# Empty half-steps before the turnings of gated values, later transpositions for block 0, and parts beside a unit's first product with V

## The chip, the cores and the metric

The kernel runs on one core of a Trainium2 chip. The metric is the device time of one execution in microseconds, as a median of runs. Below, PE is the matrix engine, PEld its weight loads, DVE the vector engine, ACT the scalar engine, POOL the general engine, and SP the engine that issues the DMAs.

## The reference

One layer: an adaptive layer norm, attention with 32 query heads and one shared key and value head of 16 columns, and a gated feed-forward. S is 2048, D is 512, F is 1792, all in float32.

```python
mod = (silu(c) @ w_mod)               # six rows of 512: sa, ca, ga, sb, cb, gb
h = layernorm(x) * (1 + ca) + sa
q, k, v = h @ wq, h @ wk, h @ wv      # 32 heads of 16; one k, one v of 16
p = softmax(q @ k.T / 4)              # per head, 2048 x 2048
x = x + ga * ((p @ v) @ wo)
h = layernorm(x) * (1 + cb) + sb
x = x + gb * ((sigmoid(h @ w_gate) * (h @ w_up)) @ w_down)
```

## The kernel before

**Units and half-steps.** After a prologue of some 108 us, attention runs in 32 units: 8 blocks of 256 queries times 4 groups of 8 heads. A unit has 16 steps, one for each block of 128 keys, and a step has two half-steps. So the loop has 1024 half-steps. Half-step 12 of unit 5 is written 5.12 below. In each half-step PE makes, in the order `ORDER`, two score tiles for the row maxima (`a0`, `a1`, tile `sa`), two transposed score tiles (`s0`, `s1`, tile `st`), and the product of an older block's exponentials with V (`c`, tile `craw`), which runs `LAG` = 2 steps behind. DVE reduces both `sa` tiles to maxima (`mx`), and ACT takes the exponential of both `st` tiles (`P`). The maxima run 84 products ahead of the scores, so the last 42 half-steps have none. `sa` has three buffers and `st` has two. Every matmul of the loop uses a piece of the array of 64 rows by 32 columns, and pieces on both halves of the rows run side by side.

**Parts.** All other matrix work of the layer is cut into parts and put at the end of half-steps: the rest of the queries (`q`), the output projection (`wo`), the gate and up products (`gu`) and the down product (`dn`). A part is one term of a pair of product groups (`Couple`): eight matmuls of 64x32 with 512 columns. A pair of gate and up groups has 24 parts. `places` spreads the parts of a `Couple` over half-steps at a rate, with a weight for each half-step from `weight`. A unit's last product with V stands in half-step 3 of the next unit; ACT then copies `craw` out into `cs`, and the first product of the new unit, in half-step 4, waits for that copy. `weight` gives half-step 3 five parts (`SWAP`) and half-step 4 none, but only for couples at the full rate. Query parts and the parts of block 0 (those marked `slow`) have the same weight everywhere.

**Blocks.** The feed-forward goes by 4 blocks of 512 rows. Block 0 is done in two halves of 256 rows in units 4 to 16, at the lower rate `ERATE`. There the gate and up products come out row-wise (`pgr`). ACT takes the tanh of one part of them, DVE copies the other part, POOL multiplies them into `g`, and a `Turned` piece of four transpositions by PE turns `g` for the down product. Block 0 has 14 of these turnings (stage `gt`). `Transposes` (stage `tr`) turn the normed rows `t` into `h2` before the gate and up products. `pick` takes the next group: a `tr` may start `GAP` steps after the norm was recorded in `marks`, and couples in `spare` fill in where the main list can't go on. When a `Couple` doesn't fit before the end of the loop, it stays over for the tail. The tail follows the last half-step. It does the leftover couples and block 3's feed-forward without attention, with whole-array matmuls (line 185).

**Order on the engines.** PE, DVE, ACT and SP work in the order in which the code is written until the tail. POOL's order is chosen by the scheduler when the kernel is built.

Of the kernel before, what the change touches and what calls it, by code (L numbers as in the profile page):

```python
# [26 lines left out]
NKB = S // P  # L27
# [34 lines left out]

SKIP = 9
GAP = 2
KEPT = 2
RATE = 2.2
QRATE = 1.0
ERATE = 1.65
MOST = 3
SWAP = 5  # L70
WSTEPS = 95
WLAST = 112
WLATE = 2
# [14 lines left out]
def adaln_mqa_glu_kernel(  # L88
# [47 lines left out]
    pinned, first = [True], [True]  # L136
# [50 lines left out]
                self.end(self.bank, False)  # L187

    class Couple:
        slow = False  # L190

        def __init__(self, a, c):
            self.gs, self.stage, self.w, self.n = (a, c), a.stage, a.w, 2 * a.n
# [586 lines left out]
    marks = {}  # L780
# [16 lines left out]
    def ffn_groups(b):  # L797
# [80 lines left out]
        def gu_rows(t, e):  # L878
            at = len(uses) // 2 * (t // 2) + e

            def term(n, rs):
                k, i = divmod(n, 3)
                gw = gws[at]
                h_, w_ = passes(*h2[k], 0, 1)[i]
                return h_[rs, t * P:(t + 1) * P], gw[rs, :, w_:w_ + 3:2, k, :]

            def end(p_, second):
                gs_[t, e] = g_ = t32("g")
                z = p_.rearrange("p (f m n) -> p f m n", f=2, m=2)
                th, u_ = (g_[:, m * QU:(m + 1) * QU].rearrange("p (f n) -> p f n", f=2) for m in range(2))  # L890
                act.activation(th, z[:, :, 0], AF.Tanh, scale=0.5 / (SH * SW))
                dve.tensor_copy(u_, z[:, :, 1])
                pool.tensor_scalar(th, th, 1.0, 1.0, op0=ALU.add, op1=ALU.mult)
                pool.tensor_tensor(th, th, u_, op=ALU.mult)
                marks[b, "g", t // 2, e] = now[0]

            return Group("gu", 12, "pgr", term, end, (lambda: ask(at + GWB)) if t % 2 == 0 else None)

        def turned(u, e):
            pt = bank("pt3")  # L900
            for f in range(2):
                for t in range(2):
                    pe.transpose(pt[:, (2 * f + t) * P:(2 * f + t + 1) * P], gs_[2 * u + t, e][:, f * P:(f + 1) * P], ident)
            h32, hi, lo = t32("h32"), t16("gh"), t16("gl")
            act.activation(h32, pt, AF.Identity)
            pool.tensor_scalar(hi, h32, 1.0, 0.0, op0=ALU.mult, op1=ALU.add)
            pool.tensor_tensor(lo, h32, hi, op=ALU.subtract)
            for f in range(2):
                gT[fs[2 * e + f]] = hi[:, f * QU:(f + 1) * QU], lo[:, f * QU:(f + 1) * QU]
# [30 lines left out]
        def down_group(t, lo, hi):  # L940
            n_ = hi - lo
            t0 = t % 2 if split else t

            def term(n, rs):
                f, i = fs[lo + n // 3], n % 3
                g_, w_ = passes(*gT[f], wdh, wdl)[i]
                return g_[rs, t0 * P:(t0 + 1) * P], w_[rs, f, :]

            def end(p_, second):
                ot = t32("ot")  # L950
                if second:
                    act.activation(ot, p_, AF.Identity)
                    pool.tensor_tensor(ot, ot, mods[5], op=ALU.mult)
                else:
                    dve.tensor_tensor(ot, p_, mods[5], op=ALU.mult)
                if hi < NFC:
                    pool.tensor_tensor(x1[t][0], ot, x1[t][0], op=ALU.add)
                else:
                    pool.tensor_tensor(ot, ot, x1[t][0], op=ALU.add)
                    store = lambda: sp1.dma_start(out[b * QB + t * P:b * QB + (t + 1) * P, :], ot)  # L960
                    if tail:
                        store()
                    else:
                        defer(2 + t % 2, store)

            return Group("dn", 3 * n_, "pd", term, end)
# [3 lines left out]
        if split:  # L970
            halves = []
            for u in range(2):
                gs = [Couple(gu_rows(2 * u, e), gu_rows(2 * u + 1, e)) for e in range(NFC // 2)]
                ts = [Turned(lambda n0, n1, u=u, e=e: turned(u, e), (b, "g", u, e)) for e in range(NFC // 2)]
                seq = [gs[0]]
                for e in range(1, NFC // 2):
                    seq += [gs[e], ts[e - 1]]
                seq += [ts[-1], Couple(down_group(2 * u, 0, NFC), down_group(2 * u + 1, 0, NFC))]
                for z in seq:
                    z.slow = True  # L980
                halves.append([Couple(*wos[2 * u:2 * u + 2]), trs[u], trs[u + 2], *seq])
            return halves
        gs = []
# [67 lines left out]

    def weight(hb, q):
        s, h = divmod(hb, 2)
        t = (s - LAG) % NKB
        if s >= LAG and (t, h) == (0, 0):
            return 0.0
        if (t, h) == (NKB - 1, 1):
            return SWAP / RATE if not q else 1.0  # L1060
        return 1.0 if q else (2 - SWAP / RATE + 2 * (NKB - 1)) / (2 * NKB - 2)

    def places(m, hb, rate, most, skip, part):
        ws = []
        rate, most = rate / part, most / part
        while sum(ws) * rate < m + lead[0] / part - rate / 2 or sum(ws) * most < m:
            ws.append(0.0 if len(ws) < (skip or 0) else weight(hb + len(ws), skip is not None))
        lead[0] += part * (m - rate * sum(ws))
        ends = [round(m * sum(ws[:k + 1]) / sum(ws)) for k in range(len(ws))]
        return [k - z for z, k in zip([0] + ends, ends)]  # L1070
# [3 lines left out]
    def ready(pair, gs, i):  # L1074
        for g in gs:
            g.ready = i * NKB
        return [(pair, g) for g in gs]

    def pick(s):
        if first_rows and s >= (len(units) - NU) * NKB + SKIP:  # L1080
            return first_rows.pop()
        while main and main[0][0] is None:
            n = main.pop(0)[1]
            spare.extend(z[1] for z in main[:n])
            del main[:n]
        if main:
            b, g = main[0]
            if g.stage == "tr":
                ok = (b, g.u) in marks and s >= marks[b, g.u] + GAP
            elif g.stage == "wo":  # L1090
                ok = s >= g.ready + SKIP
            elif g.stage == "gt":
                ok = s >= marks[g.mark] + GAP + 1
            else:
                ok = not spare
            if ok:
                return main.pop(0)[1]
        return spare.pop(0) if spare else None


    def plan(s, hb):
        if run:
            return
        g = pick(s)
        if g is None:
            lead[0] = 0.0
            return
        if g.stage in ("tr", "gt"):
            sizes = [4]
        else:  # L1110
            q = g.stage == "q" and s < FIRST
            light = g.slow
            rate, most = (QRATE, 1) if q else (ERATE, 2) if light else (RATE, MOST)
            sizes = []
            for leg in range(2):
                sizes += places(g.n // 2, hb + len(sizes), rate, most, (3 if leg == 0 else 0) if q else 0 if light else None, g.w)
            if hb + len(sizes) > 2 * len(units) * NKB:
                spare.insert(0, g)
                return
        at = 0  # L1120
        for z in sizes:
            run.append((g, at, at + z))
            at += z
        assert at == g.n, (at, g.n, g.stage)

    def piece(s, h):
        plan(s, 2 * s + h)
        if run:
            g, n0, n1 = run.pop(0)
            if n1 > n0:  # L1130
                g.part(n0, n1)
# [5 lines left out]
    for i, (b, o) in enumerate(units):  # L1137
        if o == 0 and b == NQ - 1:
            ends = ffn_groups(NB - 1)
            first_rows.append(Couple(*ends[0][:2]))  # L1140
# [9 lines left out]
        elif o == 0 and b % 2 == 0 and b > 0:  # L1150
            wos, trs, gs = blocks.pop(b // 2 - 1)
            gs = [Couple(*wos[2:]), trs[1], trs[3], *gs]
            main.extend([*ready(b // 2 - 1, gs[:-KEPT], i), (None, KEPT), *ready(b // 2 - 1, gs[-KEPT:], i)])
        for kb in range(NKB):
            s = i * NKB + kb
# [29 lines left out]
            while wdone < nw:  # L1185
                if wdone < nw - 4 and (wdone + 0.5) * WSTEPS > (s + 1) * (nw - 4):
                    break
# [23 lines left out]
    wos, trs, gs = ends  # L1211
# [44 lines left out]
```

## Time and profile before

| | us |
|---|---|
| median of 3 runs (lowest, highest) | 1713.26 (1713.11, 1713.76) |
| the profiled execution, its own time | 1710.52 |
| the profile's span | 1708.7 |
| PE, DVE, ACT, POOL busy | 1656.0, 1430.7, 1299.5, 605.8 |
| mean granted PE clock | 0.990 |
| copies `cs` that end the units: first and last start | 156.5, 1571.9 |
| row maxima on DVE, 2048 of them | 1287.6 |
| exponentials on ACT, 2048 of them | 1171.4 |

The span leaves out 1.8 us of the profiled execution's own time, and that execution is 2.7 us under the median. A busy PE is not always a PE at its peak: a matmul's record holds its latency (376 ns for the f16 ones) and not only its share of the array, so neighbouring records overlap.

### The profile page before, as it was taken

The page shows a single profiled execution, that of the slowest core. Times are in us where ns is not written, and L with a number is a line of the kernel's source. Part 1 is how long each engine was busy: PE and PEld are TensorE (multiplying, and loading weights), DVE is VectorE, ACT ScalarE, POOL GpSimd, SP SyncE. Part 2 cuts the span into 40 slices and gives each one's busy share as a digit, 9 for nine tenths or more (in the row PEclk, how much of TensorE's full clock was granted, in tenths as well). Part 3 has the DMA queues.
Part 4 walks back from the last instruction along what each step waited for, and adds up shares of the span by engine and source line. Part 5 has one row for each costly group of instructions (what it writes and reads, how often), then busy time and mean ns, then how long its engine had stood idle before and what let it go on. Part 6 is the DMA issues. An engine that isn't in the chain of part 4 may idle for free.

```text
span 1708.7 us, 89331 instructions
## 1 busy us (share of the span) xinstructions
PE 1656.0 (97%) x40446; PEld 1000.3 (59%) x40446; DVE 1430.7 (84%) x2440; ACT 1299.5 (76%) x2361; POOL 605.8 (35%) x808
## 2 busy tenths in 40 slices
PE   6999999999999999999999999999999999999998
PEld 3335555456656656666656666666666676654443
DVE  7799999989999999999999999999999999931411
ACT  5449998878888888888888888888888888885100
POOL 4433556753423022233143322232443232322423
PEclk9989999999999999999999999999999999999999
DMA  7112333422210022210021110111121100111211
GB/s 242 53 61 61 124 116 112 142 71 69 82 52 15 16 77 64 64 27 16 28 73 40 40 37 14 38 39 28 40 77 40 56 24 25 35 54 48 74 49 50
DMA packets 88184, 101.48 MB, mean 59 GB/s; under 512 B 24580, under 2 KB 65532, under 8 KB 87804
## 3 DMA queue, kind: packets, MB, share of 16 engines
q1 hardware_dynamic: 87804, 95.78, 17.6%
q8 instruction: 316, 5.18, 1.3%
q14 instruction: 64, 0.52, 0.1%
HBM read 75.16 MB, written 16.24 MB: 53 GB/s over the span
## 4 chain that ended last, share of the span: by engine, by line
PE 84%; DVE 7%; ACT 3%; POOL 2%; DMA 1%; issue 1%; SPq 1%; POOLq 0%; ACTq 0%; DVEq 0%
PE craw L134 23%; PE sa L134 14%; PE st L134 12%; PE pgu L134 10%; PE pd L134 7%; PE pgr L134 5%; PE pgu L185 4%; DVE mx L134 4%; PE pd L185 3%; PE pq L134 2%; PE po L134 2%; ACT P L134 1%; PE pt L134 1%; SPq L134 1%; DVE h2h L134 1%
## 5 line engine op out<-in xcount | busy, mean ns | idle before, releaser
L134 DVE TENSOR_REDUCE mx<-sa 128x1 f32<-128x512 f32 x2048 | 1287.6, 682 | 85.3 <-PE st L134 43.6
L134 ACT ACTIVATE P<-st 128x512 f32<-128x512 f32 x2048 | 1171.4, 598 | 215.3 <-PE st L134 153.2
L134 PE MATMUL craw<-P,V 64*32 64x512 f32 x8192 | 1098.6, 600 | 1.1 <-ACT cs L134 0.3
L134 PE MATMUL sa<-kp,qp 64*32 64x512 f16 (+1 forms) x7940 | 838.2, 379 | 11.8 <-DVE mx L134 10.9
L134 PE MATMUL st<-qp,kp 64*32 64x512 f16 x8192 | 838.9, 380 | 7.6 <-ACT P L134 6.3
L134 PEld LDWEIGHTS <-kp 64*32 64x32 f16 x8192 | 334.5, 91 | 210.2 <-issue 79.6
L134 PEld LDWEIGHTS <-qp 64*32 64x32 f16 (+1 forms) x7940 | 279.2, 92 | 152.1 <-issue 74.8
L134 PEld LDWEIGHTS craw<-P,V 64*32 64x32 f32 x8192 | 184.4, 105 | 28.5 <-ACT cs L134 6.9
L134 PE MATMUL pgu<-h2h,gw 64*32 64x512 f16 x3584 | 195.4, 376 | 0.7
L134 PE MATMUL craw<-nought 64*32 64x1 f16 x1046 | 170.6, 163 | 0.0
L134 PEld LDWEIGHTS <-gw 64*32 64x32 f16 x5376 | 123.3, 92 | 44.7 <-issue 15.7
L134 PEld LDWEIGHTS <-nought 64*32 64x32 f16 x1046 | 97.4, 93 | 70.4 <-issue 48.7
L134 PE MATMUL pgu<-h2l,gw 64*32 64x512 f16 x1792 | 122.6, 376 | 0.0
L557 POOL MEMSET qp<- 32x1024 f16 x60 | 56.7, 944 | 146.0 <-PE st L134 127.5
L920 POOL TENSOR_SCALAR th<-th 128x512 f32<-128x512 f32 x28 | 17.3, 617 | 251.8 <-ACT th L134 231.5
L134 PE MATMUL pgr<-gw,h2h 64*32 64x512 f16 x1792 | 104.3, 377 | 0.5 <-DVE g L134 0.5
L134 PE MATMUL pd<-wdl,gh 64*32 64x512 f16 x1152 | 77.9, 376 | 0.0
L134 PE MATMUL pd<-wdh,gh 64*32 64x512 f16 x1152 | 75.9, 376 | 0.0
L134 PE MATMUL pd<-wdh,gl 64*32 64x512 f16 x1152 | 75.6, 376 | 0.0
L321 POOL TENSOR_SCALAR wst<-wst 128x512 f32<-128x512 f32 x46 | 28.6, 621 | 127.3 <-DMA wst<-in_B_w_up_dram 64.4
L914 ACT ACTIVATE th<-pgu 128x512 f32<-128x512 f32 x14 | 8.4, 597 | 82.0 <-PE pgu L185 82.0
L185 PE MATMUL pgu<-h2h,gw 128*128 128x512 f16 x224 | 67.0, 379 | 1.5 <-DVE h2h L356 1.5
(173 smaller groups left out, 1624.7 us busy)
## 6 DMA issues: line engine op xcount, KB each, us to landing
gw<-wD SPq DMA_DIRECT2D x35, 1024.0 KB
wD<-gw SPq DMA_DIRECT2D x14, 512.0 KB
wm<-in_w_mod_dram SPq DMA_DIRECT2D x6, 1024.0 KB
qp<-qD SPq DMA_DIRECT2D x192, 32.0 KB
qD<-q SPq DMA_DIRECT2D x16, 256.0 KB
xr<-in_A_x_dram SPq DMA_DIRECT2D x16, 256.0 KB
out_dram<-ot SPq DMA_DIRECT2D x16, 256.0 KB
raw<-cs SPq DMA_DIRECT2D x248, 16.0 KB
```

Source lines behind the costliest of these rows:

```text
L134: return (lambda *a, **k: keep(f_(*a, **k))) if pinned else f_
L185: pe.matmul(cut[0](self.bank) if cut else self.bank, l_, r_, start=(n == 0), stop=(n == self.n - 1))
L321: pool.tensor_scalar(w_, w_, SW, 0.0, op0=ALU.mult, op1=ALU.add)
L557: eng.memset(qp[j:j + 32], 0.0)
L914: act.activation(th, p_, AF.Tanh, scale=0.5 / (SH * SW))
L920: pool.tensor_scalar(th, th, 1.0, 1.0, op0=ALU.add, op1=ALU.mult)
```

## The change

It touches the planner alone; the arithmetic and the work are the same.

```diff
+SLOWGAP = 5
-ERATE = 1.65
+ERATE = 1.9
+FRESH = 0.9
...
     class Couple:
-        slow = False
+        slow = first = False
...
                 for z in seq:
                     z.slow = True
+                gs[0].first = True
...
-    def weight(hb, q):
+    def weight(hb, rate):
         s, h = divmod(hb, 2)
         t = (s - LAG) % NKB
         if s >= LAG and (t, h) == (0, 0):
-            return 0.0
+            return FRESH
         if (t, h) == (NKB - 1, 1):
-            return SWAP / RATE if not q else 1.0
-        return 1.0 if q else (2 - SWAP / RATE + 2 * (NKB - 1)) / (2 * NKB - 2)
+            return SWAP / rate
+        return (2 * NKB - FRESH - SWAP / rate) / (2 * NKB - 2)

     def places(m, hb, rate, most, skip, part):
-        ws = []
+        ws, full = [], rate
...
-            ws.append(0.0 if len(ws) < (skip or 0) else weight(hb + len(ws), skip is not None))
+            ws.append(0.0 if len(ws) < (skip or 0) else weight(hb + len(ws), full))
...
             if g.stage == "tr":
-                ok = (b, g.u) in marks and s >= marks[b, g.u] + GAP
+                ok = (b, g.u) in marks and s >= marks[b, g.u] + (GAP if b else SLOWGAP)
...
         if g.stage in ("tr", "gt"):
-            sizes = [4]
+            sizes = [4] if g.stage == "tr" else [0, 4]
         else:
...
-                sizes += places(..., (3 if leg == 0 else 0) if q else 0 if light else None, g.w)
+                sizes += places(..., 3 if leg == 0 and (q or g.first) else 0, g.w)
```

In words: each turning of gated values takes two half-steps, the first with nothing in it. Block 0's transpositions of normed rows start 5 steps after the mark in place of 2. The first gate and up couple of each half of block 0 begins with three empty half-steps. Where a couple runs there, half-step 3 of a unit has five parts (in a few units four) and half-step 4 has parts too, whatever the couple; in units 7 to 9 a turning falls into half-step 3. Block 0's rate goes from 1.65 to 1.9 parts, which brings its 24-part couples from 15 half-steps to 14 or 12.

**What it moves, at three places.** The first is on DVE, at the first transpositions of block 0 in unit 5. `mx<-sa` are the loop's row maxima, two for each half-step; `st`, `mv` belong to the norm before the transpositions; the `h2h` casts read what the transpositions give. Before:

```order
125 L134 BN_STATS st<-xr 128x6
126 L134 BN_AGGR mv<-st 128x2
127 L134 TENSOR_REDUCE mx<-sa 128x1 x14
128 L134 CAST h2h<-h_8298 128x256
129 L134 CAST h2h<-h_8304 128x256
130 L134 TENSOR_REDUCE mx<-sa 128x1 x2
131 L134 CAST h2h<-h_8345 128x256
132 L134 CAST h2h<-h_8351 128x256
133 L134 RECIPROCAL rc<-lc 128x16
```

And now:

```order
125 L136 BN_STATS st<-xr 128x6
126 L136 BN_AGGR mv<-st 128x2
127 L136 TENSOR_REDUCE mx<-sa 128x1 x16
128 L136 RECIPROCAL rc<-lc 128x16
129 L136 TENSOR_REDUCE mx<-sa 128x1 x10
130 L136 CAST h2h<-h_8491 128x256
131 L136 CAST h2h<-h_8497 128x256
132 L136 TENSOR_REDUCE mx<-sa 128x1 x2
133 L136 CAST h2h<-h_8538 128x256
134 L136 CAST h2h<-h_8544 128x256
```

Between the norm and the casts stood 14 maxima, and now there are 26: the transpositions moved six half-steps back, from 5.12 to 5.18, and the reciprocal `rc` now stands ahead of them.

The second place is on ACT, at the sixth turning of gated values, in half-step 8.28 before and 9.03 now. `g<-pgr` are the two tanh of the gate products, `P<-st` the exponentials, two for each half-step, and `h<-pt` the copy of the turned values. Before:

```order
686 L134 ACTIVATE g<-pgr 128x256 x2
687 L134 ACTIVATE P_13477<-st 128x512
688 L134 ACTIVATE P_13496<-st 128x512
689 L134 ACTIVATE h_13508<-pt_13503 128x512
690 L134 ACTIVATE P_13477<-st 128x512
```

And now, where a unit's copy `cs` happens to stand between:

```order
698 L136 ACTIVATE g<-pgr 128x256 x2
699 L136 ACTIVATE P_13665<-st 128x512
700 L136 ACTIVATE P_13684<-st 128x512
701 L136 ACTIVATE P_13665<-st 128x512
702 L136 ACTIVATE cs<-craw 128x512
703 L136 ACTIVATE P_13684<-st 128x512
704 L136 ACTIVATE h_13729<-pt_13724 128x512
```

Two exponentials stood between the products' tanh and the turned values, and now four do: one more half-step of attention, in which no part stands.

The third place is on ACT, at the end of the loop and the start of the tail. `th<-pgu` are the tanh of the gate products of the other blocks, `a` belongs to the last unit's attention, and `h<-pt2` to block 3. Before:

```order
2311 L134 ACTIVATE th<-pgu 128x512
2312 L134 ACTIVATE cs<-craw 128x512
2313 L739 ACTIVATE a<-raw 128x256
2314 L355 ACTIVATE h_49588<-pt_49581,sh,sc 128x256
2315 L355 ACTIVATE h_49594<-pt_49581,sh,sc 128x256
```

And now:

```order
2309 L136 ACTIVATE P_48951<-st 128x512
2310 L136 ACTIVATE cs<-craw 128x512
2311 L741 ACTIVATE a<-raw 128x256
2312 L916 ACTIVATE th<-pgu 128x512 x2
2313 L357 ACTIVATE h_49247<-pt_49240,sh,sc 128x256
```

Two tanh now stand behind the loop: two gate and up couples, 48 parts, went from the loop into the tail. One didn't find room at the end of unit 31, where the last 11 half-steps are empty. The other was pushed back in unit 25, where 15 half-steps, 25.11 to 25.25, are empty: a spare couple of the down product is now taken ahead of the second output projection, which puts block 2's second transpositions 11 half-steps later, and nothing else is left to fill in. The number of half-steps is unchanged, and of the parts in the loop unit 5 has 15 in place of 29, unit 6 has 54 for 48, unit 9 has 50 for 58, unit 10 has 61 for 50, unit 15 has 60 for 52 and unit 16 has 43 for 52; unit 25 has 34 for 68 and unit 31 has 48 for 72.

More of the change, by code (lines that the diff above doesn't have):

```diff
@@ L1115, in plan @@
             for leg in range(2):
-                sizes += places(g.n // 2, hb + len(sizes), rate, most, (3 if leg == 0 else 0) if q else 0 if light else None, g.w)
+                sizes += places(g.n // 2, hb + len(sizes), rate, most, 3 if leg == 0 and (q or g.first) else 0, g.w)
             if hb + len(sizes) > 2 * len(units) * NKB:
```

## The prediction

> **What bounds the kernel now.** I read the page first, then busy time by windows, the waits in the chain and in the timeline, and the tail.
>
> ```profile
> span 1708.7 us, 89331 instructions
> PE 1656.0 (97%) x40446; PEld 1000.3 (59%) x40446; DVE 1430.7 (84%) x2440; ACT 1299.5 (76%) x2361; POOL 605.8 (35%) x808
> PE   6999999999999999999999999999999999999998
> DVE  7799999989999999999999999999999999931411
> ```
>
> PE and DVE are both above 90% through the whole loop. DVE falls away where the maxima end, near 1508 us. Which of the two binds is read by unit. The windows below are unit 1 (28 query parts), unit 13 (48 parts of block 0 and two turnings) and unit 19 (70 parts at the full rate); the columns are length, then busy time and number of instructions of each engine, granted clock, DMA share.
>
> ```profile
> core 0: us, PE busy (x) PEld busy (x) DVE busy (x) ACT busy (x) POOL busy (x), PEclk, DMA share, GB/s
> 151.70:193.20 41.50, 40.67 (x1034) 22.71 (x1026) 40.67 (x69) 37.61 (x70) 25.13 (x32) 1.00 0.43 130
> ...
> 690.20:735.50 45.30, 44.57 (x1208) 27.75 (x1198) 42.04 (x73) 39.44 (x74) 11.45 (x18) 1.00 0.19 61
> ...
> 963.20:1009.40 46.20, 45.86 (x1372) 31.62 (x1364) 42.58 (x72) 38.25 (x71) 14.36 (x17) 1.00 0.16 50
> ...
> 170.47 9.80 DVE mx L134 x16
> ```
>
> With 28 parts the unit is DVE's: 40.67 of 41.50. With 48 or 70 parts neither engine is full, and the 22 parts between units 13 and 19 cost only 0.9 us, 0.04 each; the 20 between units 1 and 13 cost at most 3.8 us, 0.19 each, turnings included. Sixteen maxima in a row take 9.80, so DVE's floor is 9.80 / 8 = 1.23 us a half-step, against 46.20 / 32 = 1.44 at the full rate. So a part in the loop lies mostly beside DVE's work, and a removed wait is a gain only as far as DVE was short of work.
>
> **The change part by part.** The sum is made against the profiled execution's 1710.52 us.
>
> *A. The first transpositions, 5.12 to 5.18.* The rows are POOL's, PE's and the windows around them.
>
> ```profile
> 336.71 0.62 POOL L321 TENSOR_SCALAR wst<-wst 128x512 f32<-128x512 f32 x1 [3.33 <-DMA wst<-in_B_w_down_dram]
> 341.19 2.08 POOL L351 TENSOR_SCALAR t<-xr,mv,rs 128x512 f32<-128x512 f32 x1
> ...
> 337.99 0.33 PE L134 MATMUL pt<-ident,t 128*128 128x128 f32 x1
> 343.33 0.90 PE L134 MATMUL pt<-ident,t 128*128 128x128 f32 x3 [5.01 <-POOL t L351]
> ...
> 338.00:343.30 5.30, 0.32 (x10) 0.12 (x1) 1.09 (x2) 0.69 (x2) 4.76 (x9) 0.93 1.00 378
> 343.30:347.00 3.70, 3.67 (x32) 1.80 (x32) 1.93 (x4) 2.13 (x4) 1.92 (x3) 0.50 0.06 15
> 347.00:351.00 4.00, 4.00 (x87) 2.17 (x91) 3.16 (x8) 2.98 (x6) 3.26 (x5) 0.70 0.09 21
> ```
>
> POOL waits 3.33 us for a weight, and the second normed row `t` is queued behind that weight, so it ends at 343.27. PE stands 5.0 us in front of the transposition, with the loop's scores queued behind it. Afterwards the clock is 0.50 for 3.7 us and 0.70 for 4.0 us, a loss of 3.7 x 0.50 + 4.0 x 0.30 = 3.05 us of PE. By PE the wait costs 5.0 + 3.05 = 8.1. By DVE, which is busy 92% in unit 19 and here 1.09 + 1.93 + 3.16 = 6.18 of 13.0, it costs 13.0 x 0.92 - 6.18 = 5.8. The Trainium skill (TensorE: Matmul & The Clock Gate, What's actually happening) says that the clock is halved after an idle window of about 3.4 us and whole again after about as long at work; by it the loss after the wait would be 3.4 x 0.5 = 1.7 and the PE figure 6.7. The trace shows the halving, but for longer. The same page gives a rule against empty stretches; here unit 1, with 28 parts, has clock 1.00, so the empty half-steps don't bring it on.
>
> Six half-steps at DVE's floor are 7.4 us, so PE comes to the transposition near 345.4, 2.1 us behind `t`. The weight that holds POOL is issued behind unit 5's own DMAs, so it moves with the unit's start and this margin stays. I take -6.5; bounds -3.5 (part of the wait comes back further on, rival 2) and -8.1.
>
> *B. The turnings.* Here one with a wait, then one where a half-step already lay between (the last turning of each half; two of the 14).
>
> ```profile
> 713.60 0.16 PE L134 MATMUL craw<-nought 64*32 64x1 f16 x1
> 714.29 0.63 PE L134 MATMUL pt<-ident,g 128*128 128x128 f32 x4 [0.34 <-POOL g L893]
> ...
> 764.78 0.16 PE L134 MATMUL craw<-nought 64*32 64x1 f16 x1
> 764.89 0.66 PE L134 MATMUL pt<-ident,g 128*128 128x128 f32 x4
> ...
> L134 PE MATMUL pt<-ident,g 128*128 128x128 f32 x56 | 8.8, 281 | 4.2 <-POOL g L893 2.8 <-DVE g L134 1.3
> ```
>
> From the last matmul ahead of it the turning starts 0.69 us later with the wait and 0.11 without: 0.58 a turning, 7.0 for the 12. The row named for the wait, POOL's `g`, was written a couple earlier; what is late is a free bank, which ACT and DVE still read from the couple just ended. An empty half-step of 1.23 us or more covers that. The parts it displaces go to the other half-steps of the couple, at 0.04 to 0.19 each. Since DVE fills 42.04 of the 45.30, not all of it can be gained: -4, between -2 and -7.
>
> *C. Half-steps 3 and 4.* In a unit of block 0 as it is:
>
> ```profile
> 695.91 0.60 ACT L134 ACTIVATE cs<-craw 128x512 f32<-128x512 f32 x1 [0.16 <-PE craw L134]
> 696.55 0.63 PE L134 MATMUL craw<-P,V 64*32 64x512 f32 x4
> 697.75 2.49 DVE L134 TENSOR_REDUCE mx<-sa 128x1 f32<-128x512 f32 x4 [0.56 <-PE st L134]
> ...
> 968.69 0.69 DVE L134 TENSOR_REDUCE mx<-sa 128x1 f32<-128x512 f32 x1 [0.41 <-PE craw L134]
> 969.90 1.89 DVE L134 TENSOR_REDUCE mx<-sa 128x1 f32<-128x512 f32 x3 [0.52 <-PE sa L134]
> ```
>
> PE's first product with V (696.55) waits for the copy `cs`, which ends at 696.51, and DVE is short by 0.56 behind it. The last two rows are of unit 19, which already has five parts in half-step 3: DVE is short by 0.41 + 0.52 = 0.93 there. Eleven units of queries and of block 0 get four or five parts there (units 7 to 9 get a turning, 5 and 11 nothing). If they come to look like unit 19, they lose 11 x 0.37 = 4.1. But some 3.5 parts a unit leave other half-steps for this one, 38 in all, worth 1.5 to 7.2 at 0.04 to 0.19 each. In the 13 full-rate units two parts come into half-step 4, which was empty, and leave others: even. I take 0, between -3 and +4.
>
> *D. Forty-eight parts go from the loop to the tail.* The tail's rows:
>
> ```profile
> 1572.58 1.99 PE pr L732 x8
> 1574.57 7.77 PE pd L185 x36
> 1594.65 41.60 PE pgu L185 x192
> ...
> 1577.38 0.43 DVE L740 TENSOR_TENSOR a<-raw,a 128x256 f16<-128x256 f32 x1 [0.48 <-ACT a L739]
> ...
> 1548.90:1563.40 14.50, 14.41 (x379) 7.60 (x367) 0.69 (x1) 12.84 (x23) 3.67 (x4) 1.00 0.01 3
> ```
>
> In the tail a matmul takes 41.60 / 192 = 0.217 us and nothing lies beside it: 48 x 0.217 = +10.4. What covers the last unit's division (from `pr`'s end at 1574.57 to 1577.81) was a down product of 7.77 us; now it is two gate groups, 24 x 0.217 = 5.2, still longer than 3.2. In the loop, unit 25 gets 15 half-steps without parts, 1.23 against 1.44: -15 x 0.21 = -3.2; its transpositions bring DVE work, so -3. The last 11 half-steps lose their parts and a tanh; they have no maxima and took 14.50, of which ACT was busy 12.84, one tanh (0.6) included. ACT's floor is 12.2, so at most -2.3; -2. Net +5.4, between +4.5 and +10.4 (the loop gives nothing back).
>
> *E. Parts that move between units.* Unit 5 loses 14, and units 6, 10 and 15 gain 25 from it and from units 9 and 16. At 0.04 to 0.19 each: +1, between -1.5 and +3.
>
> Sum: -6.5 - 4.0 + 0 + 5.4 + 1.0 = -4.1, so 1706.4 for the profiled execution. That one was 2.74 under the median, and the median goes to 1713.26 - 4.1 = 1709.2.
>
> **The rivals.**
>
> *1. The parts in half-steps 3 and 4 come on top (slower).* PE is at most three `sa` buffers ahead of DVE, and five parts are 5 x 0.217 = 1.1 us. If the 11 units lose unit 19's 0.37 more and get nothing back for it, and if in the 13 full-rate units the two parts in half-step 4 (0.43), where PE used to catch up, lengthen the shortage by as much, C is 4.1 + 5.6 = 9.7 and the change +5.6: 1718.9. For it: the price of a part elsewhere is as low as 0.04, so little comes back. Against it: PE's time for the parts that left is freed in those half-steps all the same. It decides the sign once C is over 4.1. Chance 0.15, its smaller sizes included.
>
> *2. The wait moves.* The low halves `h2l` that the first gate couple reads come from POOL too:
>
> ```profile
> 344.91 0.77 POOL L321 TENSOR_SCALAR wst<-wst 128x512 f32<-128x512 f32 x1 [1.64 <-DMA wst<-in_B_w_down_dram]
> 347.58 2.68 POOL L357 TENSOR_TENSOR h2l<-h,h2h 128x256 f16<-128x256 f32 x4
> ...
> 349.66 0.43 SPq L134 DMA_DIRECT2D wst<-in_B_w_down_dram  x1
> ```
>
> In the new order POOL has one more weight ahead of `h2l`, the one that SP issues at 349.66 behind the reciprocal `rc`. The reciprocal now stands ahead of the casts and needn't wait for them, and three empty half-steps follow the transpositions, so I expect that weight in time. If it comes late by what A gains, A shrinks to -1.5 and the change to +0.9: 1714.2, no change. Chance 0.12.
>
> *3. The empty half-step does nothing.* If what is late at a turning is `g` after all, or DVE is the bound there, B is 0, and the sum is -0.1: 1713.2. The two turnings without a wait speak against it. Chance 0.12.
>
> *4. PE binds more than I read.* Then B and A come out whole, -7 and -8.1, and D's loop gives back as I have it: -4.1 - 3 - 1.6 = -8.7, 1704.6. Chance 0.11.
>
> **How the numbers follow.** My forecast has 0.50, with 1709.2 and some 4 us to either side from the bounds of A, B, D and E, 1705 to 1713.5. The range reaches to rival 4 and beyond, and to the smaller sizes of rival 1: 1702 to 1717; it leaves out rival 1 at its full price and the ends of the others. A measurement here tells about 0.2%, 3.4 us, from no change. Faster by more than that (under 1709.8): somewhat over half of the forecast, 0.29, rival 4's 0.11, and 0.10 from rivals 2 and 3 and from a C at its good end: 0.50. Slower (over 1716.7): most of rival 1, 0.12, and 0.08 where D is at its upper end with B at its lower: 0.20. Within: 0.30.
>
> **What would show it.** A: no wait of PE for `t` in unit 5, a clock of 1.00 there, and unit 5 some 6 us shorter. B: 0.11 between the last matmul and each turning. C: DVE's shortage in half-steps 3 and 4 of the eleven units under 0.9, and less of it in their other half-steps. D: 48 more whole-array `pgu` matmuls between `pr` and block 3's transpositions, a tail 10.4 us longer, unit 25 some 3 us shorter. It is wrong if the loop ends less than 10.4 us earlier than before, for then the tail eats the gain, or if a new wait for POOL stands in unit 5.

## The result, and the profile after

The changed kernel takes 1712.97 us as a median (1709.62 to 1721.99). The kernel before, run beside it on the same chip, takes 1713.74 (1708.45 to 1715.41). The ratio is 1.0008, with a 95% interval of 0.9997 to 1.0018: no difference that the measurement can tell. It is made of all twenty runs of each (their means are 1714.24 and 1712.92) and is not the quotient of the two medians, which lie the other way. The forecast was 1709.2 and a gain of 4.1; by the ratio the change costs 1.4 (-0.5 to +3.1), so the sum came out 5.5 us too low.

One execution differs from the next by more than that: 1708 to 1715 for the kernel before. The profiled execution after took 1716.93, high in its spread, while the one before (1710.52) was low. So the profiles are compared here stage by stage, and ratios carry the totals. The head of the page after:

```profile
span 1715.1 us, 88626 instructions
PE 1664.1 (97%) x40113; PEld 1002.6 (58%) x40113; DVE 1428.2 (83%) x2440; ACT 1301.1 (76%) x2361; POOL 602.9 (35%) x804
PEclk9889999999999999999999999999999999999999
```

Next, busy time by windows of the changed kernel: the stretch up to the first transpositions and behind them (unit 5), unit 13, units 6 to 16 together, unit 25, and the last half-steps of the loop. The columns are those of the prediction.

```profile
321.20:343.00 21.80, 21.74 (x414) 9.15 (x411) 21.73 (x40) 19.32 (x35) 17.21 (x26) 1.00 0.40 134
343.00:350.00 7.00, 6.57 (x117) 2.82 (x117) 5.90 (x11) 5.68 (x12) 3.72 (x5) 1.00 0.36 110
690.10:736.20 46.10, 45.23 (x1221) 28.70 (x1227) 42.96 (x74) 40.17 (x75) 13.69 (x22) 1.00 0.18 59
367.00:871.50 504.50, 493.07 (x13391) 310.79 (x13388) 470.22 (x797) 432.55 (x792) 142.81 (x202) 0.99 0.15 47
1240.30:1286.50 46.20, 45.53 (x1097) 25.09 (x1095) 43.84 (x79) 39.52 (x74) 21.16 (x30) 1.00 0.22 71
1541.00:1558.00 17.00, 15.72 (x286) 5.81 (x270) 0.69 (x1) 15.80 (x29) 3.67 (x4) 1.00 0.28 94
```

Unit 5 no longer has a hole: PE is busy for 21.74 of 21.80 us, and the clock is 1.00 where it was 0.50 to 0.70. The unit takes 45.8 us in place of 52.3. Unit 25, without parts for 15 half-steps, takes 46.2 in place of 48.9. Units 6 to 16 take 504.5; the same eleven units of the kernel before:

```profile
373.50:871.70 498.20, 489.15 (x13250) 305.58 (x13242) 467.67 (x795) 429.13 (x790) 138.03 (x197) 1.00 0.15 45
```

So in these two executions 6.3 of the 6.5 us that unit 5 gives are gone again by unit 17. Of the 6.3, 3.2 lie in unit 11 (47.4 before, 50.6 now). Counted from the traces, the eleven units hold 561 parts in place of 543, but the loss doesn't follow them: units 6 and 10, with six and eleven more, take the time that they took before, unit 7, with as many, takes 0.9 more, and unit 11 has two fewer. The tail is read from the chain that ended last, first of the kernel before, then of the changed one; columns are start, length, engine, tile, line and count.

```profile
1564.49 4.00 PE po L185 x18
```

```profile
1558.46 3.99 PE po L187 x18
1566.62 3.68 PE pr L734 x8
1570.30 6.91 PE pgu L187 x32
1578.50 3.45 PE pgu L187 x16
```

The loop ends 6.0 us earlier (first `po`), but from there to the end of the span it takes 156.6 in place of 144.2: the 48 moved matmuls, which stand here as `pgu` x32 and x16 (10.36 us), and `pr`, which takes 3.68 where it took 1.99, at a granted clock of 0.84 (the window below). The slow `pr` comes and goes with the execution, not with the parts: with the same two couples in the tail it takes 3.41 in e4 below, 1.99 to 2.00 in e2, e3, e6 and e8, and with none there 3.58 in e1.

```profile
1564.00:1575.00 11.00, 10.14 (x48) 5.08 (x41) 2.61 (x3) 1.51 (x3) 0.00 (x0) 0.84 0.01 1
```

### The profile page after: what moved, and what is told of

Same layout as the page of the kernel before. It is cut to its first block, busy times and chain, and to the rows that moved or that the text cites. A ratio compares the mean times of both kernels' runs of the same rounds, so it can differ in the third digit from the quotient of the medians.

```text
span 1715.1 us, 88626 instructions
## 1 busy us (share of the span) xinstructions
PE 1664.1 (97%) x40113; PEld 1002.6 (58%) x40113; DVE 1428.2 (83%) x2440; ACT 1301.1 (76%) x2361; POOL 602.9 (35%) x804
## 4 chain that ended last, share of the span: by engine, by line
PE 84%; DVE 8%; ACT 4%; issue 1%; SPq 1%; DMA 1%; POOL 0%; POOLq 0%; ACTq 0%; DVEq 0%
PE craw L136 22%; PE sa L136 14%; PE st L136 12%; PE pgu L136 10%; PE pd L136 7%; DVE mx L136 5%; PE pgr L136 5%; PE pgu L187 5%; PE pd L187 3%; PE pq L136 2%; PE po L136 2%; ACT P L136 2%; SPq L136 1%; PE pt L136 1%; DVE h2h L136 1%
## 5 line engine op out<-in xcount | busy, mean ns | idle before, releaser
L136 PEld LDWEIGHTS <-qp 64*32 64x32 f16 (+1 forms) x7940 | 283.7, 92 | 163.4 <-issue 83.8
L136 PEld LDWEIGHTS craw<-P,V 64*32 64x32 f32 x8192 | 180.9, 105 | 18.2 <-PE craw L136 5.4
L136 PE MATMUL pgu<-h2h,gw 64*32 64x512 f16 x3328 | 186.2, 376 | 0.6
L136 PEld LDWEIGHTS <-gw 64*32 64x32 f16 x4992 | 115.9, 92 | 39.8 <-issue 14.4
L136 PE MATMUL pgu<-h2l,gw 64*32 64x512 f16 x1664 | 113.8, 376 | 0.0
L187 PE MATMUL pgu<-h2h,gw 128*128 128x512 f16 x256 | 76.6, 379 | 1.5 <-DVE h2h L358 1.5
```

The lines of the kernel that those rows point to most:

```text
L136: return (lambda *a, **k: keep(f_(*a, **k))) if pinned else f_
L187: pe.matmul(cut[0](self.bank) if cut else self.bank, l_, r_, start=(n == 0), stop=(n == self.n - 1))
```

## The experiments

Every ratio below is against the kernel before, on the same chip. A ratio of 0.001 is 1.7 us. Each experiment has 6 to 12 runs. The expectations for e9, e11 and e12 call the stretch from 17 to 30 "units 17 to 31": their times, 646.9 and 647.9, end where unit 31 begins.

| kernel | median, us | ratio | interval |
|---|---|---|---|
| changed kernel | 1712.97 | 1.0008 | 0.9997 to 1.0018 |
| e1_hold | 1707.54 | 0.9967 | 0.9953 to 0.9981 |
| e2_first0 | 1713.91 | 0.9999 | 0.9985 to 1.0014 |
| e3_no_empty | 1714.60 | 1.0010 | 1.0000 to 1.0020 |
| e4_slowgap2 | 1718.38 | 1.0036 | 1.0023 to 1.0048 |
| e5_a_alone | 1713.66 | 0.9998 | 0.9985 to 1.0011 |
| e6_oldw | 1713.45 | 1.0007 | 0.9992 to 1.0023 |
| e7_hold_no_empty | 1707.50 | 0.9963 | 0.9948 to 0.9978 |
| e8_two_in_tail | 1721.36 | 1.0041 | 1.0025 to 1.0058 |
| e9_fresh_off_full | 1711.83 | 1.0004 | 0.9991 to 1.0017 |
| e10_hold_slowgap2 | 1713.98 | 1.0006 | 0.9997 to 1.0015 |
| e11_later_and_fresh | 1703.24 | 0.9946 | 0.9931 to 0.9960 |
| e12_before_again | 1712.19 | 0.9997 | 0.9984 to 1.0011 |

### The 48 parts in the tail: e1_hold and e8_two_in_tail

The first keeps the changed kernel's parts in the loop: no spare couple is taken in the two steps before block 2's output projection. The second does the opposite to the kernel before: it leaves two couples for the tail.

```diff
+        if main and main[0][0] == 2 and main[0][1].stage == 'wo' and s >= main[0][1].ready + SKIP - 2:
+            return None
         return spare.pop(0) if spare else None
```

> The changed kernel with one line more in pick: in front of block 2's second output projection no spare couple is taken for two steps. Up to 24.15 the parts stand as in the changed kernel; behind it unit 25 keeps 66 parts in place of 34, unit 31 69 in place of 48, and no couple is left over for the tail. Theory 1 (the 48 parts in the tail ate the gain): 7 us faster than the changed kernel (tail 10.4 + 2 shorter, the loop 4 to 5 longer), 0.995 to 0.997 of the kernel before. Rival (the loop gave back what the tail took; the loss lies in block 0's units): within 2 us of the changed kernel, 0.999 to 1.002 of the kernel before.

```diff
-            if hb + len(sizes) > 2 * len(units) * NKB:
+            if hb + len(sizes) > 2 * len(units) * NKB - 20:
```

> The kernel before, but a couple that would end in the last 20 half-steps is left for the tail: the last two gate and up couples, 48 parts, go there, and the last 22 half-steps have none. Theory 1: the tail costs 10.4 us and the last half-steps give back 3 to 4 (22 x 0.1 and two tanh), so 6.5 to 8 us slower than the kernel before (1.004 to 1.005), the more if the clock is halved behind the loop (1.7). Rival (the loop gives back what the tail takes): within 2 us of the kernel before.

The hold brings the change from 1.0008 to 0.9967, 7.0 us; the two couples in the tail cost the kernel before 7.0 us (1.0041). Tails in the two chains, e1 and then e8, whose spans are 1708.2 and 1716.5:

```profile
1562.26 3.99 PE po L187 x18
```

```profile
1561.78 4.01 PE po L185 x18
```

These are 145.9 and 154.7 us. Without e1's slow `pr` (3.58 against 1.99 in e8) they lie 10.4 apart, the price of the 48 matmuls. Moving the parts costs 7 us net, from both sides.

### The empty half-step: e3_no_empty and e7_hold_no_empty

The changed kernel without the empty half-step ahead of a turning, and the same with the hold.

```diff
-            sizes = [4] if g.stage == "tr" else [0, 4]
+            sizes = [4]
```

> The changed kernel without the empty half-step in front of a turning; all else is as changed, 48 parts in the tail too. Forecast's reason B (PE's wait at a turning is lost time): 4 us slower than the changed kernel. Theory 1 (the turnings are bound by what ACT and DVE do for them, and the wait only moves from the transposition to the next scores): within 1.5 us of the changed kernel, with PE's wait of 0.5 us in front of the transpositions back, and less waiting in front of st.

> The first experiment's kernel (no couple left for the tail) without the empty half-step in front of a turning. Theory 1 (the empty half-step moves PE's wait from the transposition to the scores behind it): within 1.5 us of the first experiment's kernel, 0.996 to 0.998 of the kernel before. Forecast's reason B: 4 us slower than it, 0.999.

1.0010 against 1.0008, and 0.9963 against 0.9967: in the whole time the empty half-step is worth nothing. (Its stages do differ, because other groups land elsewhere without it: in the kept traces units 6 to 16 take 4.1 us less in e3 than in the changed kernel, and unit 11, whose clock stays whole there, alone takes 4.8 less; units 17 to 30 take 2.5 more.) Groups of PE's instructions in units 6 to 8 show why. The number behind the last bar is PE's idle time just before the group, with what ended it. The kernel before, the changed kernel, and e3:

```profile
L134 PE MATMUL st<-qp,kp 64*32 64x512 f16 x772 | 78.6, 378 | 0.3 <-ACT P L134 0.3
L134 PE MATMUL pt<-ident,g 128*128 128x128 f32 x24 | 3.8, 279 | 2.1 <-POOL g L893 1.8 <-DVE g L134 0.4
```

```profile
L136 PE MATMUL st<-qp,kp 64*32 64x512 f16 x768 | 78.4, 378 | 2.2 <-ACT P L136 2.2
L136 PE MATMUL pt<-ident,g 128*128 128x128 f32 x20 | 3.3, 287 | 0.0
```

```profile
L136 PE MATMUL st<-qp,kp 64*32 64x512 f16 x764 | 78.0, 378 | 0.2 <-ACT P L136 0.2
L136 PE MATMUL pt<-ident,g 128*128 128x128 f32 x28 | 4.4, 281 | 2.3 <-POOL g L895 2.3
```

The 2.1 us in front of `pt` are gone and 2.2 us stand in front of `st`. The first of these waits, in rows of ACT and PE of the changed kernel:

```profile
392.85 0.65 ACT L136 ACTIVATE g<-pgr 128x256 f32<-128x256 f32 x2
393.37 1.71 ACT L136 ACTIVATE P<-st 128x512 f32<-128x512 f32 x3
394.04 0.40 PE L136 MATMUL st<-qp,kp 64*32 64x512 f16 x4 [0.43 <-ACT P L136]
395.21 0.66 PE L136 MATMUL pt<-ident,g 128*128 128x128 f32 x4
395.96 0.60 ACT L136 ACTIVATE h<-pt 128x512 f32<-128x512 f32 x1
```

The wait stands in the empty half-step itself, 1.17 us ahead of the transposition. It ends with an exponential that stands on ACT behind the two tanh of the gate products, 0.52 us after their start. The copy `h` comes 1.9 us after the wait and has no part in it. Twelve of the fourteen turnings show these rows in this order. PE's waits in units 6 to 16, in the kernel before in front of `pt`, then in the changed kernel in front of `st`:

```profile
PE pt L134 <- POOL g L893: 2.8, 8, 0.4
PE pt L134 <- DVE g L134: 1.3, 4, 0.4
PE st L136 <- ACT P L136: 6.0, 14, 0.5
```

The columns are the total in us, how often, and the longest. So 4.1 us of waits became 6.0, of which 5.5 stand at the twelve turnings. The wait moved, and it did not get smaller.

### The later transpositions: e4_slowgap2, e10_hold_slowgap2, e5_a_alone

`SLOWGAP = 2` puts block 0's transpositions back to 5.12, in the changed kernel (e4) and in e1 (e10). The kernel e5 is the kernel before with `SLOWGAP = 5` and `ERATE` 1.7, which keeps all parts in the loop.

```diff
-SLOWGAP = 5
+SLOWGAP = 2
```

> The changed kernel with block 0's transpositions 2 steps behind the mark, as before, in place of 5; the rest as changed. If reason A holds, the wait of 5 us for the normed row and the half clock behind it are back in unit 5 (some 52 us in place of 45.8) and the kernel is 5 to 7 us slower than the changed one, 1.003 to 1.005 of the kernel before, unless unit 11, whose transpositions now fall some 7 half-steps earlier, keeps its clock and gives 3 us back. If the wait costs only what DVE loses: 2 to 4 slower.

> This is the first experiment's kernel (hold, all parts in the loop, empty half-steps kept; ratio 0.9967), with block 0's transpositions back at 5.12. If the later transpositions are worth what the changed kernel showed for them (4.8 us when taken back, 6.5 in unit 5): unit 5 takes 51 to 53 us with a half clock behind POOL's late row, and the ratio is 0.999 to 1.001. If the gain of unit 5 is given back further on, as the run with the later transpositions alone would have it: ratio 0.995 to 0.998.

```diff
-                ok = (b, g.u) in marks and s >= marks[b, g.u] + GAP
+                ok = (b, g.u) in marks and s >= marks[b, g.u] + (GAP if b else SLOWGAP)
```

> The kernel before with block 0's transpositions 5 steps behind the mark in place of 2, and nothing else of the change; block 0's rate is 1.7 in place of 1.65, so that every couple still ends inside the loop. Theory 1 (the transpositions are the one gain of the change): 6 us faster than the kernel before, 0.996 to 0.9975, as fast as the first experiment's kernel, which has the rest of the change too. Rival (the turnings or the parts in half-steps 3 and 4 bring something): 2 us or more slower than that kernel, over 0.998.

Taken back, the transpositions cost 4.8 us in the changed kernel and 6.7 with the hold (1.0006 against 0.9967). The timeline of PE in e10, and then its window behind the wait, show the hole again, 4.70 us and a clock of 0.56:

```profile
342.94 0.90 PE L136 MATMUL pt<-ident,t 128*128 128x128 f32 x3 [4.70 <-POOL t L353]
```

```profile
342.80:350.00 7.20, 7.06 (x81) 3.04 (x83) 4.22 (x9) 4.78 (x9) 3.63 (x6) 0.56 0.12 31
```

But e5 was a miss: the later transpositions alone gave 0.9998. Its unit 5 did shrink (44.6 us), and the loss came in units 17 to 30. Here are these units in e5, in e9 and e7 of the next group, and last in the kernel before:

```profile
866.80:1522.50 655.70, 646.04 (x18726) 433.22 (x18715) 594.97 (x996) 542.24 (x986) 212.39 (x262) 1.00 0.13 41
```

```profile
866.00:1519.50 653.50, 646.71 (x18722) 430.10 (x18725) 596.01 (x996) 541.99 (x985) 210.21 (x260) 1.00 0.14 41
```

```profile
865.20:1512.10 646.90, 642.01 (x18705) 433.63 (x18702) 592.45 (x996) 542.46 (x984) 209.28 (x260) 1.00 0.14 41
```

```profile
871.70:1519.60 647.90, 642.88 (x18720) 430.45 (x18715) 595.07 (x995) 542.06 (x985) 210.53 (x260) 1.00 0.13 41
```

In e5 DVE and ACT are busy as long as before; PE has 9.66 us idle in place of 5.02, and is busy 3.2 longer with the same work. The next group of experiments looks for the cause.

### The parts in half-step 4: e6_oldw, e9_fresh_off_full, e11_later_and_fresh

The change gives half-step 4 parts in two kinds of units. e6 takes the new weights away from queries and block 0; e9 takes half-step 4 away from the couples at the full rate (in e7); e11 is the kernel before with `SLOWGAP = 5`, the hold, `ERATE` 1.8 and the full rate's parts in half-step 4.

```diff
-            return FRESH
+            return FRESH if rate == RATE else 1.0
...
-            return SWAP / rate
+            return SWAP / rate if rate == RATE else 1.0
+        if rate != RATE:
+            return 1.0
```

> The changed kernel with the weights of half-steps 3 and 4 as before for query parts and block 0 (one weight everywhere); at the full rate half-step 4 keeps its 0.9. The loop has the same number of parts, 48 stay in the tail. Forecast's reason C (one shortage of DVE takes the place of the other): within 1.5 us of the changed kernel. Rival 1 of the forecast (five parts come on top): 4 us faster than the changed kernel.

```diff
-            return FRESH
+            return 0.0 if rate == RATE else FRESH
...
-        return (2 * NKB - FRESH - SWAP / rate) / (2 * NKB - 2)
+        return (2 * NKB - (0.0 if rate == RATE else FRESH) - SWAP / rate) / (2 * NKB - 2)
```

> This is the version without empty half-steps and with the hold (1707.5 us, ratio 0.9963), but the couples at the full rate leave half-step 4 of a unit empty again, as the kernel before does; the parts of block 0 keep theirs, and all parts stay in the loop. Theory F, that the later transpositions alone gave nothing because the parts in half-step 4 at the full rate carry the other half of the gain: ratio 0.999 to 1.001, units 17 to 31 take 653 us or more in place of 646.9. Theory S, that the missing gain was lost in stalls of PE that no wait explains and that come and go with the order: ratio 0.995 to 0.998, units 17 to 31 at 646 to 650 us.

```diff
-            return 0.0
+            return 0.0 if q else FRESH
...
-        return 1.0 if q else (2 - SWAP / RATE + 2 * (NKB - 1)) / (2 * NKB - 2)
+        return 1.0 if q else (2 * NKB - FRESH - SWAP / RATE) / (2 * NKB - 2)
```

> The kernel before with three things: block 0's transpositions 5 steps behind the mark, parts in half-step 4 for couples at the full rate, and the hold that keeps all parts in the loop (block 0's rate 1.8 for the same end). No empty half-steps and no other weights for queries and block 0. Theory F: ratio 0.995 to 0.998. Theory S: the same, if no stall comes; units 17 to 31 tell: 646 to 650 us with less than 2 us of unexplained PE stalls. If something else of the change carries the gain (its weights for block 0, its three empty half-steps): ratio 0.999 to 1.001.

For queries and block 0 the new weights do nothing (1.0007 against 1.0008). At the full rate the gain hangs on them, once the transpositions are late: without them e7 falls from 0.9963 to 1.0004 (7 us, as theory F has it), and with them, the hold and a rate of 1.8 e5 goes from 0.9998 to 0.9946 (8.9 us). With the transpositions early they bring nothing: e10 has them and stands at 1.0006. e11 is the fastest kernel of the study, 9.3 us ahead of the kernel before. Units 20 to 23, with 282 or 283 parts in each kernel, show it in windows of the kernel before, e9, e7 and e11:

```profile
1009.40:1193.70 184.30, 183.69 (x5487) 125.88 (x5486) 171.29 (x283) 154.35 (x278) 50.42 (x58) 1.00 0.10 29
```

```profile
1006.00:1190.10 184.10, 183.28 (x5485) 124.56 (x5485) 171.14 (x283) 153.80 (x279) 51.46 (x57) 1.00 0.10 29
```

```profile
1003.30:1186.10 182.80, 182.29 (x5484) 127.49 (x5474) 169.76 (x283) 153.60 (x279) 49.85 (x56) 1.00 0.10 29
```

```profile
1000.60:1183.30 182.70, 182.08 (x5482) 128.18 (x5474) 169.50 (x283) 153.52 (x279) 49.96 (x56) 1.00 0.10 29
```

With half-step 4 empty the four units take 184.1 to 184.3, with parts in it 182.7 to 182.8: some 0.37 a unit. DVE has 283 instructions in each, but its busy time is 1.4 to 1.8 less while its idle time stays near 13. That fits maxima that more often follow each other without a pause: 16 in a row are charged 9.80, 0.61 each, and a single record 0.68. The other full-rate units don't carry this on. Units 17 to 30 take 646.9 in e7, and 647.8 to 647.9 in the kernel before, which has half-step 4 empty too; units 17 to 19 alone take 137.7 there, 138.2 in e7, and 140.0 in e9 and in e11. So parts in half-step 4 are not what parts e9 and e5 from the kernel before, and why those two need 653.5 and 655.7 is not shown.

### The second half clock: e2_first0

Three empty half-steps only for the first half of block 0 (unit 5), not for the second (unit 11).

```diff
-                gs[0].first = True
+                gs[0].first = u == 0
```

> The changed kernel, but the three empty half-steps stand in front of the first gate and up couple of block 0's first half alone (unit 5), not of its second (unit 11). Theory 1 (PE runs short of work behind the transpositions of unit 11, and its clock is halved for some 6 us): unit 11 takes 47 to 48 us in place of 50.6, clock 1.00 in it, 3 us faster than the changed kernel. Rival (the loss in unit 11 is DVE's four casts, which stand there in both kernels): unit 11 stays near 50 us, and the time is that of the changed kernel.

A half-miss: the half clock in unit 11 is gone, but the unit takes 50.0 us all the same, with five more parts; the time, 0.9999, is 1.5 us under the changed kernel's, within both intervals. The windows of the changed kernel in unit 11, at the second transpositions of block 0, one of e2 at the same place, and then rows of PE's timeline in the changed kernel:

```profile
593.70:601.20 7.50, 5.92 (x99) 2.40 (x84) 7.37 (x11) 6.66 (x14) 7.38 (x8) 0.97 0.19 72
601.20:608.40 7.20, 6.96 (x111) 3.75 (x111) 5.39 (x10) 3.44 (x6) 0.75 (x2) 0.55 0.08 17
```

```profile
591.20:598.70 7.50, 5.96 (x111) 2.68 (x96) 7.37 (x12) 6.55 (x14) 7.38 (x9) 1.00 0.32 79
```

```profile
598.85 0.40 PE L136 MATMUL sa<-kp,qp 64*32 64x512 f16 x4 [0.87 <-DVE mx L136]
601.44 0.61 PE L136 MATMUL sa<-kp,qp 64*32 64x512 f16 x4 [0.90 <-DVE mx L136]
```

DVE has four casts `h2h` beside its maxima there, PE waits for it twice, and with no parts to fill in PE is busy for 5.92 of 7.50. Then the clock is halved for 6.8 us. A busy share of 79% doesn't bring this on by itself: e2, with like waits (0.88 and 0.70), is busy for 5.96 of 7.50 and the kernel before for 6.09 (597.8 to 605.3), and both keep a clock of 1.00. They have 111 and 115 matmuls in that time, the changed kernel 99. In e1, whose order is the same up to there, the clock is halved for 3.4 us and unit 11 takes 48.5.

### The kernel before once more: e12_before_again

> The kernel before, unchanged. Ratio 1.000, its interval within 0.9985 to 1.0015; a second profile of the same order, which tells how much of a unit's time differs from one execution to the next: I expect units 17 to 31 within 3 us of 647.9 and unit 5 within 1 us of 52.3, and PE stalls without a wait, none of which the first profile had in units 26 to 30, in some of them.

Ratio 0.9997, and the same unit times: unit 5 takes 52.3, units 17 to 30 take 647.8. Its profiled execution was 4.0 us longer than the first one. Three us of it are waits of PE, in units 2, 4 and 7, that end with nothing recorded; the first execution has none up to unit 16. From the waits of PE between 108 and 875 us:

```profile
PE craw L134 <- issue: 1.7, 2, 1.0
PE sa L134 <- issue: 1.3, 1, 1.3
```

The columns are the total in us, how often, and the longest.

## Why the prediction was right or wrong

The measured median lies inside the range of 1702 to 1717 and 3.8 over the forecast. The sum behind the forecast doesn't deserve that: it was 5.5 us off against the ratio, its gain didn't come, and it is the width of the range that holds the result. The prediction's own sign against itself also came true, a loop that ends less than 10.4 us earlier: it ended 6.0 earlier.

**A, later transpositions: right.** Unit 5 lost 6.5 us (52.3 to 45.8), the forecast's value; that it agrees to the digit is luck, since the unit takes 44.0 to 44.8 in the eight experiments that keep the later transpositions. Taking them back cost 4.8 and 6.7 in the ratios. No wait for `t` is left, and rival 2's new wait for POOL did not come.

**B, the empty half-step: the step that failed.** "An empty half-step of 1.23 us or more covers that" took a wait that is no longer at the turning for a wait that is gone. I had read the wait as one for a free bank, which no run shows or refutes, and overlooked what ACT's work on the couple just ended does to PE's scores: in the empty half-step the two tanh put off the exponentials, and PE waits in front of `st` as long as it had waited in front of `pt`. The size was too large as well: the row that the prediction shows has 4.2 us of waits in front of `pt` for all turnings, and not 7. Rival 3 gave B = 0, though for another reason. e3 and e7 show the 0.

**C, half-steps 3 and 4: 0 was right for queries and block 0, and at the full rate near enough in the changed kernel itself.** There units 17 to 30 without unit 25 took 1.7 us less than before, for a forecast of "even". Only between e7 and e9 does the same edit weigh 7 us, and no price of the prediction, which argued from parts that change places, could give that.

**D, parts in the tail: right in its rows, small in its sum.** The 10.4 came (10.36 in the two `pgu` rows), unit 25 gave 2.7 of 3, and the stretch from unit 31 to the tail 1.4 of 2. The 1.7 at `pr` belong to that execution. Net 7 by e1 and e8, against 5.4.

**E, parts moved among units: mis-sized.** Units 6 to 16 grew by 6.3 us in the profiled execution, not by 1 less the 4 of B. Unit 11, with two parts fewer and a half clock, makes 3.2 of it, and 1.6 are stalls of PE that nothing recorded ends (the last section has them), of which the kernel before has none up to there. The parts themselves cost little, as forecast: units 6 and 10 hold 17 more between them and take no longer. In e1 and e2, which have much the same order there, the eleven units grow by 4.5 and 4.3.

**The clock.** The sentence that "the empty half-steps don't bring it on" was wrong. Unit 1 was no guide for unit 11, where DVE has casts besides. The rows above show a clock of 0.55 after a stretch in which PE was busy for 79% and no single wait reached 1 us, and a whole clock in e2, without the three empty half-steps there. The Trainium skill (TensorE: Matmul & The Clock Gate, A second HAM failure mode: psum-queue depth-cycling) tells of a PE whose frequent short idle times between groups of matmuls throttle it; this trace agrees for unit 11, though e2 and the kernel before, busy for as large a share, keep their clock, so no run here shows how much idle time it takes. I had weighed only the page's rule on one long idle window.

**The sum.** By the two profiled executions the change costs 6.4 us, 10.5 more than forecast: B and E together missed by 9.3 (units 6 to 16), D by 2.9 and C at the full rate by -1.7. The ratio says 1.4, so some 5 of this belong to the two executions. Parts of it can be named: 1.7 at `pr`, the 1.6 of stalls, and the 2.1 by which unit 11 is longer than in e1. With one trace of each kernel it isn't shown how the rest divides.

**What stays open.** A and C at the full rate together make 0.9963 to 0.9946. Each without the other, in e5, e9 and e10, makes 0.9998 to 1.0006, though neither needs the other by any wait that I found. The parts in half-step 4 can't be the whole reason, since the kernel before does without them in units 17 to 30 and loses nothing there. Theory S of the expectations puts the missing gain down to stalls of PE that no wait explains. Part of it is named by the waits of PE in units 17 to 30: e5 lost 4.8 us to waits that nothing recorded ends (`issue`; the three rows of e5's waits added), while the kernel before lost none there.

```profile
PE pgu L135 <- issue: 2.1, 3, 1.2
PE craw L135 <- issue: 1.6, 3, 1.0
PE sa L135 <- issue: 1.1, 2, 0.6
```

In e10 these waits are 3.2, in e9 1.5, in e11 2.7, in e7 1.4. They don't sort the kernels, so theory S explains e5 in part and the others not. The last section shows what these stalls follow.

## What to carry to other kernels

When you add a pause to remove a wait, look at what the other engines do in the pause: here ACT's two tanh held up PE's next scores for as long as PE had waited at the transposition, and the wait stood in the pause itself. A planner's edit also decides what doesn't fit: here 48 parts that fell out of the loop cost 7 us, as much as the best part of the change gained, and two lines in `pick` kept them in. Test the parts of such a change in pairs as well as alone, since two edits that are worth some 7 us each when one is taken out of the pair gave 0 without the other and 6 to 9 together.

## What the runs showed of the hardware

PE stops for up to 1.7 us, with no semaphore wait that the profile can name, behind a 1 MB weight load. The rows are from the windows and then the PE timeline of e11 in unit 18; the load `gw<-wD` was issued at 918.81.

```profile
920.00:923.00 3.00, 3.00 (x98) 2.04 (x86) 2.58 (x5) 2.34 (x5) 0.00 (x0) 1.00 0.91 315
923.00:926.50 3.50, 2.47 (x82) 1.48 (x73) 2.07 (x5) 1.90 (x4) 0.00 (x0) 1.00 0.36 95
```

```profile
925.96 0.39 PE L136 MATMUL pgu<-h2l,gw 64*32 64x512 f16 x1 [1.03 <-issue]
```

The DMA share is 0.91 at 315 GB/s, and then PE is idle for 1.03 in the middle of a part. Such stalls recur behind the same load, in unit 18 of eleven of the fourteen traces and in units 7, 26 and 27 of six each, and differ between executions. In the loops of the fourteen traces there are 59 of over 0.3 us, and 54 of them stand 5.5 to 8.5 us behind the issue of a `gw` load.

The profile's queue `q8`, kind "instruction", shows what they follow. It carries packets of 16 KB: 316 for the 80892 matmuls and weight loads of the kernel before, and 314 for the 80226 of the changed kernel, one for every 256. In e11 packets start at 907.9, 912.8 and 916.4, and the next only at 923.5, when the load is nearly through; the stall ends 2.5 us after that. All 59 stalls end 2.2 to 2.8 us after the start of a packet, and for 58 of them that packet started 346 to 452 PE instructions after the one before it, where 253 are usual. That fits a PE that runs out of instructions while their packet stands behind the load. Not every late packet has this effect: 186 were as late, and two of three passed without such a stall. The Trainium skill (Runtime: NRT & Kernel Launch, Instruction fetch mechanics) has that fetch on a DMA queue of its own and calls its cost mostly hidden. These traces agree for most of the 4278 packets in the loops and show the exception. No run moved a load to test it.
